# Top-32 attention and a two-layer MLP on one core: weights decoded through a PSUM bank, another cut of the last batch, new priorities

## The chip, the cores and the metric

One Trainium2 chip, one of its cores. The metric is the device time of one execution in microseconds (us), the median of three runs. The core's engines are TensorE (PE), VectorE (DVE), ScalarE (ACT), GpSimd (POOL) and SyncE (SP, which here only issues transfers); each runs its own instructions in their order, and an instruction that must wait holds up all behind it on its engine.

## What is computed

Attention over 4 batches, 8 heads, 576 positions of 64 numbers, in which each query keeps its 32 highest scores; the result, 2304 tokens of 512, goes through two matrices with h * sigmoid(h) between them. All inputs of the attention are fp32; the two weight matrices come as 64-bit floats, for the factor that scales them makes them so.

```python
def _attn_ref(q, k, v):
    scores = scale * np.matmul(q, k.transpose(0, 1, 3, 2))
    kth = np.partition(scores, -top_k, axis=-1)[..., -top_k:-top_k + 1]
    mask = scores >= kth
    scores = np.where(mask, scores, -1000000000.0)
    scores = scores - np.max(scores, axis=-1, keepdims=True)
    attn = np.exp(scores)
    attn = attn / (np.sum(attn, axis=-1, keepdims=True) + 1e-09)
    return np.matmul(attn, v).astype(np.float32)
...
def _moe_ref(x, w_in, w_out):      # x: 2304 x 512, w_in: 512 x 2048, w_out: 2048 x 512
    h = x @ w_in
    g = h * (1.0 / (1.0 + np.exp(-h)))
    return (g @ w_out).astype(np.float32)
```

## The kernel before

**Attention.** Heads go in pairs (four per batch, `pr`). A group is a batch's stretch of query blocks for one pair (`CUTS`: blocks i0 to i1 of 128 queries, and a tail of 64 or not). A tile is 128 queries of one head against 576 keys, 144 tiles in all. For each tile TensorE makes the scores in two halves (L489, or L493 and L494 from batch 1 on), ScalarE copies them to SBUF (L511), VectorE takes the eight highest of each 72 (L577, eight times), thins them to a pivot (L593, L600), ScalarE (L614, L618) and GpSimd (L617) use the pivot to build a row whose eight highest (L619, VectorE) hold the 32nd score. ScalarE makes the exponentials (L534), VectorE masks them and sums them (L540), TensorE transposes them (L644) and, once per chunk of up to 320 queries, multiplies them with the values (L731). VectorE multiplies that with the inverse sums (L739, called the product of a chunk here), ScalarE casts the result to a shortened fp32 (L758) and GpSimd subtracts that from the full one (L270), so that both parts go into the MLP.

**MLP.** The 2304 tokens are nine blocks of 256. A block can start when all four pairs' chunks that cover it have gone through L758 and L270: block 0 needs the first four products L739, block 1 the first eight. For each of the 16 slices of 128 hidden columns TensorE makes three products of 256 columns four times (L798, L799, L800), ScalarE tanh (L804), VectorE the product with h (L807), ScalarE and GpSimd the two parts (L810, L270), and TensorE three products of 512 columns twice (L837 to L839) into two accumulator banks of PSUM (`accs`, banks 6 and 7). Blocks 7 and 8 run together at the end, since batch 3's last group covers both.

**The decode of weights.** Both matrices are 16 tiles each of 128 x 512 64-bit numbers: 32 tiles, loaded by SP (L330). A tile's numbers are pairs of 32-bit words, a low and a high one (`lo_`, `hi_`). The wanted fp32 bits are sign and exponent and 20 bits of mantissa from the high word shifted left by three, and three more bits from the low word. `POOL_SIGN`, a word of 32 bits, picks for each tile one of two ways. For 24 tiles ScalarE turns the low word's upper half into a number near 2 whose last bits are the wanted ones (L348), takes the sign of the high word (L351), GpSimd multiplies the two (L352) and VectorE joins the shifted high word to it by exclusive or (L343). For 8 tiles VectorE shifts and masks (L367) and joins sign and low bits in two further passes (L343 twice). Behind either, ScalarE casts the fp32 tile to its high part (L379) and GpSimd subtracts (L270). Block 0 reads w_in from these tiles; for later blocks each two slices are stored to memory and loaded again by SP.

```python
op("act:dec", 0.565, low, r=[("r", key)], w=[("g", key)], use=[br] + ub)
op("act:sgn", 0.56, ..., r=[("g", key)], w=[("sg", key)], use=[br, bm])
op("pool:sgn", 1.22, ..., r=[("g", key), ("sg", key)], w=[("t1", key)], use=[bm, br])
op("dve:dec+", 0.602, lambda: stt(hi_(), 3, ALU.logical_shift_left, ALU.bitwise_xor), r=[("t1", key)], w=[("t2", key)], use=[bm, br])
```

**What sets the order.** `Schedule` holds all operations with a planned cost, what they read and write, and the buffers they use; `run` plays them through and writes each engine's instructions in the order in which the plan starts them. Where several are ready on an engine at once the one with the lowest priority number goes first: its tile's number plus an entry of `TUNE` for its kind. PSUM banks and SBUF buffers are given out in the plan too: the kinds `sp` (scores), `tp` (transposes), `h` and `pv` share banks 0 to 5 (`ANY`), and `LIMIT` bounds how many buffers of a kind live at once. A kind that ends in `+`, and GpSimd's own kinds, may not overlap in the plan.

A second emission (`general=True`) stands in a branch that is taken only if a check at the end fails; it does not run here. That check reads both matrices again (L907, L911, L915 on VectorE) behind the attention.

## Time and profile before

| | |
|---|---|
| runs, us | 778.66, 778.24, 777.57; median 778.24 |
| the profiled execution, us | 778.45, its span 776.7 |
| busy us of the span | PE 708.6, DVE 670.4, ACT 634.8, POOL 556.7 |
| busy share | PE 91%, DVE 86%, ACT 82%, POOL 72% |
| chain that ended last, by engine | PE 66%, DVE 17%, ACT 8%, issue 3%, POOL 2%, DMA 2% |
[...]

The busy shares are means over stretches that differ: in the first fortieth parts of the span TensorE is busy two to three tenths, from the eleventh on nearly all the time, while VectorE, ScalarE and GpSimd thin out in the last fifth, where the MLP of the last two blocks is left. TensorE's products overlap, so a TensorE that is shown busy is not for that at its peak. [...]

### The profile page before, as it was taken

Reading aid. Unit: us, or ns where it says so; the run is one execution under the profiler, and the core shown is the slowest. Engines: PE = TensorE matmul, PEld = TensorE weight load, DVE = VectorE, ACT = ScalarE, POOL = GpSimd, SP = SyncE. Lnnn points to the kernel's source line nnn. Section 1 sums busy time; section 2 is a strip of 40 time slices with the busy share of each in tenths; the row PEclk is TensorE's granted clock in tenths of the full one; section 3 lists DMA queues with packets and bytes.
Section 4 is the critical chain, followed back from the end, with each engine's and each line's share of the span. In section 5 each row is a group of like instructions: output and inputs, shape, how many; then the busy total and the mean of one; then the engine's idle time right before and its main releaser. Section 6 shows DMA issues by size and latency. Waiting matters only on the chain.

```text
span 776.7 us, 15935 instructions
## 1 busy us (share of the span) xinstructions
PE 708.6 (91%) x4802; PEld 589.8 (76%) x4802; DVE 670.4 (86%) x2931; ACT 634.8 (82%) x1602; POOL 556.7 (72%) x567
## 2 busy tenths in 40 slices
PE   2327789988999999999999999999999999999996
PEld 2214558865888887788978888888888888899995
DVE  4999999987999998999999989799997888769920
ACT  6888998997999989999989999999979898232222
POOL 7999889999998668787866878777776565222221
PEclk8656799999999999999999999999999999999999
DMA  8804342346754335434642454354323343989701
GB/s 316 299 1 133 120 169 67 138 183 253 290 201 159 128 95 195 158 107 162 221 143 89 158 176 151 112 188 170 138 76 122 144 166 135 385 318 343 289 1 60
DMA packets 41600, 131.29 MB, mean 169 GB/s; under 512 B 9504, under 2 KB 15648, under 8 KB 33312
## 3 DMA queue, kind: packets, MB, share of 16 engines
q1 hardware_dynamic: 41504, 130.17, 46.7%
q8 instruction: 40, 0.66, 0.3%
q14 instruction: 56, 0.46, 0.2%
HBM read 117.05 MB, written 13.11 MB: 168 GB/s over the span
## 4 chain that ended last, share of the span: by engine, by line
PE 66%; DVE 17%; ACT 8%; issue 3%; POOL 2%; DMA 2%; SPq 1%; ACTq 0%; POOLq 0%; DVEq 0%
PE bank L731 8%; PE bank L798 7%; PE bank L799 7%; PE bank L800 7%; PE acc L837 7%; PE bank L644 7%; PE acc L839 6%; PE acc L838 6%; DVE cand L577 4%; PE bank L493 3%; PE bank L494 3%; DVE kth L619 3%; DVE p L540 3%; DVE tg L343 2%; PE bank L491 2%
## 5 line engine op out<-in xcount | busy, mean ns | idle before, releaser
L617 POOL TENSOR_TENSOR s<-s,s 128x576 f32<-128x576 f32 x144 | 217.8, 1513 | 48.0 <-ACT s L614 46.9
L577 DVE MAX8 cand<-s 128x8 f32<-128x72 f32 x1152 | 203.3, 218 | 22.1 <-ACT s L511 21.7
L270 POOL TENSOR_TENSOR gg<-tg,gg 128x512 fp32r<-128x512 f32 (+1 forms) x73 | 98.6, 1352 | 102.3 <-ACT gg L810 101.6
L798 PE MATMUL bank<-big,big 128*128 128x256 f32 x576 | 167.2, 290 | 0.0
L800 PE MATMUL bank<-big,big 128*128 128x256 f32 x576 | 162.2, 282 | 0.2 <-POOL big L270 0.2
L799 PE MATMUL bank<-big,big 128*128 128x256 f32 x576 | 162.1, 281 | 0.0
L614 ACT ACTIVATE s<-s,piv 128x576 f32<-128x576 f32 x144 | 113.6, 789 | 10.2 <-DVE piv L593 9.5
L540 DVE SCALAR_TENSOR_TENSOR p<-s,kth,p 128x576 f32<-128x576 f32 x128 | 117.9, 927 | 3.7 <-ACT p L534 3.1
L619 DVE MAX8 kth<-s 128x8 f32<-128x583 f32 x144 | 109.3, 759 | 13.5 <-POOL s L617 12.5
L511 ACT ACTIVATE s<-bank 128x288 f32<-128x288 f32 x288 | 106.7, 426 | 12.9 <-PE bank L489 6.2
L798 PEld LDWEIGHTS bank<-big,big 128*128 128x128 f32 x576 | 109.1, 189 | 8.4 <-issue 4.2
L644 PE MATMUL bank<-ident,p 128*128 128x128 f32 x576 | 81.9, 281 | 33.9 <-DVE p L540 33.6
L799 PEld LDWEIGHTS bank<-big,big 128*128 128x128 f32 x576 | 109.4, 190 | 3.0
L800 PEld LDWEIGHTS bank<-big,big 128*128 128x128 f32 x576 | 109.1, 189 | 0.6 <-POOL big L270 0.6
L837 PE MATMUL acc<-wo,gg 128*128 128x512 f32 x256 | 109.3, 427 | 0.0
L644 PEld LDWEIGHTS bank<-ident,p 128*128 128x128 f32 x576 | 68.0, 144 | 47.4 <-DVE p L540 34.5
L839 PE MATMUL acc<-wo,gg 128*128 128x512 f32 x256 | 101.2, 395 | 1.9 <-POOL gg L270 1.8
L838 PE MATMUL acc<-wo,gg 128*128 128x512 f32 x256 | 100.8, 394 | 0.0
L534 ACT ACTIVATE p<-s,stat 128x576 f32<-128x576 f32 x128 | 98.7, 792 | 1.6 <-POOL stat L544 1.5
L731 PE MATMUL bank<-pt,s 128*64 128x256 f32 (+4 forms) x720 | 93.7, 374 | 0.0
L804 ACT ACTIVATE tg<-bank 128x512 f32<-128x512 f32 (+1 forms) x73 | 43.1, 592 | 58.9 <-PE bank L800 58.5
L656 ACT COPY pt<-bank 128x384 f32<-128x384 f32 x192 | 85.1, 487 | 6.0 <-PE bank L644 5.8
(105 smaller groups left out, 1568.0 us busy)
## 6 DMA issues: line engine op xcount, KB each, us to landing
big<-scr SPq DMA_DIRECT2D x56, 1024.0 KB, 4.9
s<-in_vx_dram SPq DMA_DIRECT2D x36, 288.0 KB, 4.6
big<-in_w_in_dram SPq DMA_DIRECT2D x16, 512.0 KB, 4.4
big<-in_w_out_dram SPq DMA_DIRECT2D x16, 512.0 KB, 6.6
scr<-big SPq DMA_DIRECT2D x8, 1024.0 KB, 4.1
p<-in_w_in_dram SPq DMA_DIRECT2D x16, 512.0 KB, 6.4
p<-in_w_out_dram SPq DMA_DIRECT2D x16, 512.0 KB, 7.0
out_dram<-tg SPq DMA_DIRECT2D x18, 256.0 KB, 2.6
```

Of the source, the lines that this page charges most:

```text
L540: nc.vector.scalar_tensor_tensor(out=x["p"], in0=x["s"], scalar=thr[e], in1=x["p"], op0=ALU.is_ge, op1=ALU.mult, accum_out=den[:, e:e + 1])
L577: nc.vector.max(out=d["cand"][:, 8 * c:8 * c + 8], in_=d["s"][:, 72 * c:72 * c + 72])
L617: op("pool:f", 1.36, lambda: nc.gpsimd.tensor_tensor(out=d["f"][:, 0:S], in0=d["f"][:, 0:S], in1=d["s"], op=ALU.mult), r=both, w=[("f", t) ...
L619: op("dve:mx8", 0.675, lambda: nc.vector.max(out=kth[:, 143 - t:151 - t], in_=d["f"][:, 0:S + 7]), r=[("f", t), ("pad", t)], w=[("thr", t) ...
L644: nc.tensor.transpose(d["tp", r][0:w, o0:o0 + 128], st[key][:, c0:c0 + w], ident)
L731: nc.tensor.matmul(ck.pv[64 * h:64 * h + 64, 0:n], v, ck.pt[:, 4 if j == 4 else 5 * h + j, 0:n], start=(j == 0), stop=(j == 4), skip_group ...
L798: nc.tensor.matmul(h, wh, x[:, 0, kk, :], start=(kk == 0), stop=False)
L799: nc.tensor.matmul(h, wh, x[:, 1, kk, :], start=False, stop=False)
L800: nc.tensor.matmul(h, wl, x[:, 0, kk, :], start=False, stop=(kk == 3))
L837: nc.tensor.matmul(a, d["gg"][:, 0, ts], wo[:, m, 0, :], start=(m == 0), stop=False)
L838: nc.tensor.matmul(a, d["gg"][:, 0, ts], wo[:, m, 1, :], start=False, stop=False)
L839: nc.tensor.matmul(a, d["gg"][:, 1, ts], wo[:, m, 0, :], start=False, stop=(m == NM - 1))
```

## The change

All 32 tiles are now decoded in one way. ScalarE writes the low word's number into a PSUM bank (kind `dec`, which may take the two accumulator banks while they are free, or any of the six shared ones), VectorE joins the shifted high word to it in the bank, and a second VectorE pass joins the sign and writes the fp32 tile to SBUF. The sign pass of ScalarE, the product of GpSimd, the shift of VectorE and `POOL_SIGN` are gone. Batch 3's queries are cut as those of batches 1 and 2, (0, 2) and (2, 4) with the tail, in place of (0, 3) and (3, 4) with the tail: a chunk of 256 and one of 320 queries per pair, where there were 256, 128 and 192. The priorities `TUNE`, the limits of buffers and three constants of the plan (`SLOP`, `DMA_SLOP`, and the general branch's `big.ro`) have other values, so the order on all engines is another throughout.

```diff
-TUNE = {"cand": 76.5, "cert": -38.5, "dec": 0.5, ... "whi": 42, "wi": 22, "wlo": 21, "wload": -20.5, "xhi": -14, "xlo": -8.5}
+TUNE = {"cand": 26.5, "cert": -30, "dec": 3.5, ... "whi": -31, "wi": -8, "wlo": 16.5, "wload": 64.5, "xhi": -36, "xlo": -2.5}
...
-CUTS = [...] + [((0, 2, False), (2, 4, True))] * (NB - 2) + [((0, 3, False), (3, 4, True))]
+CUTS = [...] + [((0, 2, False), (2, 4, True))] * (NB - 1)
...
-LIMIT = {"big.ri": 1, "big.ro": 18, "big.w": 6, "p.c": 16, "p.k": 4, "p.p": 16, "r.n": 19, "r.s": 37, "r.x": 20, "s": 6, "s.e": 40, "s.f": 4, "s.k": 1, "s.v": 1}
+LIMIT = {"big.ri": 1, "big.ro": 2, "big.w": 5, "p.c": 33, "p.k": 4, "p.p": 24, "r.n": 25, "r.s": 27, "r.x": 10, "s": 6, "s.e": 44, "s.f": 9, "s.k": 1, "s.v": 1}
...
-POOL_SIGN = 0xeff5a7ee
 ANY = [b(i) for i in range(6)]
-PSUM = dict(sp=ANY, tp=ANY, h=ANY, pv=ANY, acc0=[b(6)], acc1=[b(7)], acc2=ANY, acc3=ANY)
+PSUM = dict(dec=[b(6), b(7)] + ANY, sp=ANY, tp=ANY, h=ANY, pv=ANY, acc0=[b(6)], acc1=[b(7)], acc2=ANY, acc3=ANY)
...
-            if not general and POOL_SIGN >> 2 * m + "io".index(kind) & 1:
+            if not general:
+                bd = buf("dec", key, "dec" + kind)
+
                 def low():
                     tiles_()
-                    nc.scalar.activation(out=lo_().bitcast(F32), in_=d["r"].bitcast(U16)[:, :, 1], func=AF.Copy, scale=7.49 / 65535 * 2.0 ** -22, bias=2.0)
-
-                op("act:dec", 0.565, low, r=[("r", key)], w=[("g", key)], use=[br] + ub)
-                op("act:sgn", 0.56, lambda: nc.scalar.activation(out=d["top"], in_=hi_().bitcast(F32), func=AF.Sign), r=[("g", key)], w=[("sg", key)], use=[br, bm])
-                op("pool:sgn", 1.22, lambda: nc.gpsimd.tensor_tensor(out=d["top"], in0=d["top"], in1=lo_().bitcast(F32), op=ALU.mult), r=[("g", key), ("sg", key)], w=[("t1", key)], use=[bm, br])
-                op("dve:dec+", 0.602, lambda: stt(hi_(), 3, ALU.logical_shift_left, ALU.bitwise_xor), r=[("t1", key)], w=[("t2", key)], use=[bm, br])
+                    d["low"] = bank("dec", key)[:, 0:CW]
+                    nc.scalar.activation(out=d["low"], in_=d["r"].bitcast(U16)[:, :, 1], func=AF.Copy, scale=7.49 / 65535 * 2.0 ** -22, bias=2.0)
+
+                def join(out, scalar, op0):
+                    nc.vector.scalar_tensor_tensor(out=out.bitcast(I32), in0=hi_(), scalar=scalar, in1=d["low"].bitcast(I32), op0=op0, op1=ALU.bitwise_xor)
+
+                op("act:dec", 0.565, low, r=[("r", key)], w=[("g", key)], use=[br, bd] + ub)
+                op("dve:dec", 0.602, lambda: join(d["low"], 3, ALU.logical_shift_left), r=[("g", key)], w=[("t1", key)], use=[br, bd])
+                op("dve:dec", 0.602, lambda: join(d["top"], -0x80000000, ALU.bitwise_and), r=[("t1", key)], w=[("t2", key)], use=[bm, br, bd])
```

Lines from 400 on have a number higher by one in the kernel after (L739 is L740, L798 is L799); the decode's pass of ScalarE is L350 there, the join L353, ScalarE's cast L380, GpSimd's subtraction L269.

On VectorE, near the start of the program, the first join of before stands among the rows of the second and third tile (`cand`, `m`, `piv` and `c` are the pivot search, `kth` the 32nd score, `gg` an SBUF tile, `big` raw weights):

```order
L577 MAX cand_199<-s_169 128x8 x2
L343 SCALAR_TENSOR_TENSOR gg_160<-big_111,gg_160 128x512
L619 MAX kth<-s_185 128x8
L577 MAX cand_199<-s_169 128x8 x3
L577 MAX cand_226<-s_193 128x8
```

In the kernel after, the same place (`acc` and `bank` are PSUM banks, `p` the masked exponentials):

```order
L541 SCALAR_TENSOR_TENSOR p_206,stat<-s_125,kth,p_206 128x576
L594 MAX m_212<-c_0_217 128x8
L353 SCALAR_TENSOR_TENSOR acc_81<-big_135,acc_81 128x512
L601 MATCH_REPLACE c_0_217<-m_212,c_0_217 128x64
L353 SCALAR_TENSOR_TENSOR gg_220<-big_135,acc_81 128x512
L594 MAX piv_172<-c_0_217 128x8
L620 MAX kth<-s_215 128x8
L353 SCALAR_TENSOR_TENSOR acc_82<-big_143,acc_82 128x512
L353 SCALAR_TENSOR_TENSOR bank_78<-big_135,bank_78 128x512
L353 SCALAR_TENSOR_TENSOR gg_226<-big_143,acc_82 128x512
```

A tile's two joins stand as a pair, in and out of one bank, the first of them later than before, behind a first mask; then joins follow each other.

On VectorE, at the end of the decode before, the eighth product of a chunk (L739, `r_2156`) stands between the last joins:

```order
L343 SCALAR_TENSOR_TENSOR tg_2109<-big_2030,tg_2109 128x512
L807 SCALAR_TENSOR_TENSOR tg_2066<-tg_2066,bank_79 128x512
L600 MATCH_REPLACE c_0_2129<-m_2123,c_0_2129 128x64
L739 TENSOR_TENSOR r_2156<-bank_78,r_2028 128x256
L593 MAX piv_2161<-c_0_2129 128x8
L343 SCALAR_TENSOR_TENSOR tg_2109<-big_2030,tg_2109 128x512
L343 SCALAR_TENSOR_TENSOR gg_2121<-big_2030,gg_2121 128x512
```

After, the last joins there are these, and the eighth product (L740) stands 55 rows further down:

```order
L353 SCALAR_TENSOR_TENSOR bank_80<-big_1840,bank_80 128x512
L578 MAX cand_1912<-s_1752 128x8
L353 SCALAR_TENSOR_TENSOR tg_1928<-big_1840,bank_80 128x512
L620 MAX kth<-s_1910 128x8
L353 SCALAR_TENSOR_TENSOR bank_76<-big_1840,bank_76 128x512
L578 MAX cand_1912<-s_1752 128x8
L353 SCALAR_TENSOR_TENSOR gg_1962<-big_1840,bank_76 128x512
```

The last of the weights are joined ahead of the eighth product, no longer behind it.

Ahead of that eighth product VectorE's rows are, by line, 38 L343, 8 L367, 33 L540, 280 L577, 104 L593, 70 L600, 34 L619, 9 L697, 7 L739, 7 L807 before; after they are 64 joins, 34 masks, 293 L577, 108 L593, 72 L600, 34 L619, 9 L697, 7 L739, 8 L807 (by the numbers of before).

## Rows read from the trace of the kernel before

**Rows 1.** Busy time of each engine by stretches (start:end and length in us, then per engine busy us and number of instructions; PEclk is the granted clock as a share of full speed, here 2.4 GHz).

```profile
0.00:20.00 20.00, 5.75 (x16) 4.04 (x16) 10.21 (x57) 13.23 (x29) 14.81 (x30) 0.86 0.88 315
20.00:140.00 120.00, 79.94 (x423) 58.58 (x423) 117.79 (x473) 105.24 (x246) 113.18 (x92) 0.80 0.37 128
140.00:188.60 48.60, 43.93 (x285) 33.59 (x284) 41.40 (x168) 43.42 (x102) 46.55 (x43) 0.96 0.50 184
0.00:188.60 188.60, 129.62 (x721) 96.21 (x722) 169.40 (x696) 161.90 (x375) 174.54 (x163) 0.85 0.46 162
...
200.00:650.00 450.00, 448.63 (x3229) 378.79 (x3229) 412.45 (x2002) 423.75 (x1114) 337.70 (x366) 1.00 0.44 154
```

**Rows 2.** The chain that ended last, in order of time: start us, us, engine, what it writes, line, and how many instructions the piece holds.

```profile
29.48 0.69 DVE cand L577 x5
...
45.83 3.47 DVE tg L343 x2
...
56.37 1.76 DVE p L540 x2
...
150.56 2.58 POOL big L270 x2
```

**Rows 3.** Instructions in order of time, around the turn to token block 1 and (last two rows) two products of 512 columns late in the span: start us, us, engine, line, operation, out<-in, shapes.

```profile
188.15 0.41 DVE L739 TENSOR_TENSOR r<-bank,r 128x256 f32<-128x256 f32 x1
...
188.62 0.68 DVE L343 SCALAR_TENSOR_TENSOR tg<-big,tg 128x512 int32<-128x512 int32 x1
...
189.32 1.17 POOL L270 TENSOR_TENSOR big<-r,big 128x256 fp32r<-128x256 f32 x1 [0.57 <-ACT big L758]
...
200.06 0.28 PE L798 MATMUL bank<-big,big 128*128 128x256 f32 x1
...
758.25 0.39 PE L837 MATMUL acc<-wo,gg 128*128 128x512 f32 x1
758.47 0.39 PE L838 MATMUL acc<-wo,gg 128*128 128x512 f32 x1
```

**Rows 4.** Busy time from 0 to 200 us of the instructions of one line each, in this order: L348 and L351 (ScalarE), L352 (GpSimd), L343 and L367 (VectorE). All instances of these lines lie in the stretch.

```profile
0.00:200.00 200.00, 15.70 (x24) 0.85 0.47 167
0.00:200.00 200.00, 15.72 (x24) 0.85 0.47 167
0.00:200.00 200.00, 37.59 (x24) 0.85 0.47 167
0.00:200.00 200.00, 38.01 (x40) 0.85 0.47 167
0.00:200.00 200.00, 5.00 (x8) 0.85 0.47 167
```

**Rows 5.** Single lines (durations in ns as least/median/most), the group of L804 (busy us, mean ns), and two rows in order of time in which a join and a GpSimd subtraction run beside each other.

```profile
L807 DVE SCALAR_TENSOR_TENSOR tg<-tg,bank x73: 421/681/690, 119.5 to 765.9; 128x512 f32<-128x512 f32 x71, 128x256 f32<-128x256 f32 x2
...
L343 DVE SCALAR_TENSOR_TENSOR tg<-big,tg x22: 673/750/1892, 22.7 to 188.6; 128x512 int32<-128x512 int32 x22
...
L804 ACT ACTIVATE tg<-bank 128x512 f32<-128x512 f32 x71 | 42.4, 598 | 54.7 <-PE bank L800 54.3
...
45.83 3.46 DVE L343 SCALAR_TENSOR_TENSOR tg<-big,tg 128x512 int32<-128x512 int32 x2
...
47.02 1.72 POOL L270 TENSOR_TENSOR wo<-tg,wo 128x512 fp32r<-128x512 f32 x1
```

**Rows 6.** VectorE's groups by line from 0 to 200 us: busy us, mean ns of one | idle us before them.

```profile
L540 DVE SCALAR_TENSOR_TENSOR p<-s,kth,p 128x576 f32<-128x576 f32 x32 | 30.7, 959 | 0.4 <-ACT p L534 0.3
...
L593 DVE MAX8 m<-cand 128x8 f32<-128x64 f32 x37 | 8.0, 216 | 0.5
```

**Rows 7.** VectorE's waits, from 140 to 188.6 us and (last row) in the first 20 us: what waited, for what, total us, times, longest.

```profile
DVE tg L343 <- POOL tg L352: 1.7, 2, 1.2
DVE kth L619 <- POOL s L617: 1.6, 2, 1.2
DVE tg L807 <- ACT tg L804: 1.2, 1, 1.2
DVE cand L577 <- ACT s L511: 0.9, 1, 0.9
DVE rd L697 <- POOL rd L694: 0.6, 1, 0.6
...
DVE cand L577 <- ACT s L511: 8.9, 4, 5.0
```

**Rows 8.** The chain in order of time again: nine transposes (L644), and sets of twenty rows of L731, the weighted values of a chunk of 320, 256, 128 and 192 queries.

```profile
241.43 0.98 PE bank L644 x9
...
321.31 2.84 PE bank L731 x20
...
606.15 2.31 PE bank L731 x20
...
621.33 1.24 PE bank L731 x20
...
634.73 1.78 PE bank L731 x20
```

**Rows 9.** Instructions in order of time in the first 10 us: issues of transfers on the queue of SP, and ScalarE's first decode pass with what it waited for.

```profile
1.18 1.19 SPq L404 DMA_DIRECT2D p<-in_kx_dram  x2
...
9.00 0.67 ACT L348 ACTIVATE big<-big 128x512 f32<-128x512 uint16 x1 [1.22 <-DMA big<-in_w_out_dram]
```

More of the change, by code (lines that the diff above doesn't have):

```diff
@@ L31 @@
 W_MAX = float(np.uint32(0x47EFFFFF).view(np.float32))
-CUTS = [((0, 2, False), (2, 4, False), (4, 4, True))] + [((0, 2, False), (2, 4, True))] * (NB - 2) + [((0, 3, False), (3, 4, True))]
+CUTS = [((0, 2, False), (2, 4, False), (4, 4, True))] + [((0, 2, False), (2, 4, True))] * (NB - 1)
 SEGS = [(b, *cut) for b in range(NB) for cut in CUTS[b]]
@@ L57 @@
 PORT_DVE, PORT_POOL = 0.12, 0.05
-DMA_GO, DMA_END, FREE, SLOP, START, ALPHA = 0.65, 0.8, 0.2, 0, 1.5, 0
+DMA_GO, DMA_END, FREE, SLOP, START, ALPHA = 0.65, 0.8, 0.2, 0.05, 1.5, 0
 WINDOW = 4096 / 1.2e3
-DMA_SLOP = 3
+DMA_SLOP = 2
 GAP = {
@@ L300, in emit @@
     def emit(general):
-        own = {"s": SBUF["s"] - 5, "s.f": 1, "s.e": 1, "s.k": 1, "s.v": 2, "p.k": 4, "p.p": 2, "r.x": 1, "r.s": 1, "r.n": 1, "big.ri": 1, "big.ro": 1, "big.w": 2}
+        own = {"s": SBUF["s"] - 5, "s.f": 1, "s.e": 1, "s.k": 1, "s.v": 2, "p.k": 4, "p.p": 2, "r.x": 1, "r.s": 1, "r.n": 1, "big.ri": 1, "big.ro": 2, "big.w": 2}
         S_ = turn[0] = Schedule(own if general else LIMIT)
@@ L309, in bank @@
             i = S_.at[kind, key][0][1]
-            return banks[i]
+            return (banks + accs)[i]
         dw, wi, raws = {}, {}, {}
@@ new lines, in split_w, with mag @@
+                op("dve:dec", 0.602, lambda: join(d["low"], 3, ALU.logical_shift_left), r=[("g", key)], w=[("t1", key)], use=[br, bd])
+                op("dve:dec", 0.602, lambda: join(d["top"], -0x80000000, ALU.bitwise_and), r=[("t1", key)], w=[("t2", key)], use=[bm, br, bd])
+            else:
+                def mag():
+                    tiles_()
+                    nc.scalar.activation(out=d["top"], in_=hi_().bitcast(F32), func=AF.Abs)
+                op("act:dec", 0.48, mag, r=[("r", key)], w=[("g", key)], use=[br] + ub)
+                op("dve:dec+", 0.335, lambda: nc.vector.tensor_scalar(out=d["top"], in0=d["top"], scalar1=W_MIN, scalar2=W_MAX, op0=ALU.max, op1=ALU.min), r=[("g", key)], w=[("g1", key)], use=[bm])
@@ L363, in shl @@
                 def shl():
-                    if not general:
-                        tiles_()
                     top = d["top"].bitcast(I32)
-                    nc.vector.tensor_scalar(out=top, in0=top if general else hi_(), scalar1=3, scalar2=0x3FFFFFF8 if general else -0x40000001, op0=ALU.logical_shift_left, op1=ALU.bitwise_and)
+                    nc.vector.tensor_scalar(out=top, in0=top, scalar1=3, scalar2=0x3FFFFFF8, op0=ALU.logical_shift_left, op1=ALU.bitwise_and)
                 op("dve:dec+", 0.335, shl, r=[("g1", key), ("r", key)], w=[("t1", key)], use=[br] + ub)
-                op("dve:dec+", 0.602, lambda: stt(hi_(), -0x40000000 if general else -0x80000000, ALU.bitwise_and, ALU.bitwise_xor), r=[("t1", key)], w=[("t2", key)], use=[bm, br])
+                op("dve:dec+", 0.602, lambda: stt(hi_(), -0x40000000, ALU.bitwise_and, ALU.bitwise_xor), r=[("t1", key)], w=[("t2", key)], use=[bm, br])
```

10 lines of the change are left out of this document (2 added, 8 removed).

## The prediction

> **What bounds the kernel now.** I read the busy time by stretches first, then the chain that ended last, then the waits of single engines. The stretches [rows 1] part the span in two. From 200 to 650 us TensorE is busy 448.6 of 450 us; from there on TensorE's own work sets the pace. Up to 188.6 us it is busy 129.6 us only, while VectorE is busy 169.4, GpSimd 174.5 and ScalarE 161.9 us; from 20 to 140 us VectorE is busy 117.8 of 120. So ahead of 200 us three engines are full at once, VectorE most of all, and TensorE waits for them. The chain in order of time [rows 2] says the same: up to 60 us its long pieces are VectorE's, joins of the decode (L343) and masks (L540); from 150 us it goes over to GpSimd and ScalarE. What is gained ahead of 200 us is kept, if TensorE behind it does the same work at the same pace; what is gained later on another engine than TensorE is worth little.
>
> The point that I use as a clock is where TensorE turns to token block 1 (of 256 tokens, nine in all): its first product starts at 200.06 us [rows 3], and 576.6 us of the span of 776.7 follow. It needs the eighth product of attention and softmax sums (L739, at 188.15 us, seen by the stretch that I end at 188.6), whose cast (ScalarE) and subtraction (GpSimd) end at 190.5 (189.32 + 1.17). In the kernel before TensorE came only at 200.06 because block 0 was not done: the last join of weights but one starts at 188.62 us [rows 3], behind the eighth product, and ScalarE and GpSimd still have to split what it gives.
>
> **The change, the decode.** Before, 24 of the 32 tiles take two ScalarE passes (L348, L351), a GpSimd product (L352) and one VectorE join (L343); 8 take a shift (L367) and two joins. By their busy sums [rows 4] that is 15.7 + 15.7 = 31.4 us on ScalarE (0.65 each), 37.6 on GpSimd, 38.0 + 5.0 = 43.0 on VectorE. After, all 32 take one ScalarE pass into a PSUM bank and two VectorE joins out of it.
> - GpSimd loses 24 products: -37.6 us.
> - ScalarE: 32 passes. None of before writes PSUM; nearest are the same pass into SBUF (0.65) and L804, which reads a bank (0.598, [rows 5]). 32 x 0.65 = 20.8, so -10.6 us (-12.3 at 0.598).
> - VectorE: 64 joins. Their price decides. The 40 of before take 0.95 us each on the mean (38.0 / 40), though the faster ones take 0.67; they rise to 1.89 while GpSimd works beside them: at 45.83 us two take 3.46 us, with a GpSimd row of 1.72 us beside the second [rows 5]. The nearest row for a join with an operand in a bank is L807, 128x512 as well: 0.681 median, 0.690 at most in 73, though GpSimd is busy through most of the kernel; L807 is never slowed. I take 0.68: 64 x 0.68 = 43.5 us, +0.5 against 43.0. Lower end 0.673, the fastest join of that group of before: 43.1, nothing. Upper end 0.95, were the new joins slowed as the old ones: 60.8, +17.8. Of the ends 0.68 is the row with the nearest operands; no row writes a bank from VectorE, so the first join of each pair is the less certain.
>
> [...]
>
> **Where the time goes to.** What VectorE must do ahead of the eighth product is counted from the order: 64 joins in place of 38 joins and 8 shifts, and, moved ahead of it, 13 L577, 4 L593, 2 L600, one mask L540 and one L807. The decode is 64 x 0.68 = 43.5 against 38 x 0.95 + 5.0 = 41.1, so +2.4; the moved work is 13 x 0.14 (the piece of five in 0.69 of [rows 2]), 6 x 0.22 and 0.96 [rows 6] and 0.68, together 4.8. VectorE's work is then 169.4 + 7.2 = 176.6 us. Upon it come idle times: before, 19.2 us (188.6 - 169.4). 9.8 of these fall in the first 20 us, 2.2 up to 140, and 7.2 between 140 and 188.6 [rows 1]. Of these last, 3.9 us are waits for GpSimd (L352 itself 1.7) and 2.1 for ScalarE [rows 7], the two engines that lose 37.6 and 10.6 us of work. If they all go, 13.2 us stay; if none, 19.2. I take the middle, 16.2: part of these waits will have other causes then. The eighth product starts at 176.6 + 16.2 = 192.8; its cast and its subtraction end 2.3 us behind its start (190.49 - 188.15), so block 1 can start at 195.1 us, not 200.06: **5.0 us** earlier (8.0 to 2.0 for the ends). The last join now stands 55 rows ahead of that product on VectorE (before, behind it), so block 0 no longer sets the point. It costs nothing on the path that ScalarE and GpSimd still cast and subtract 32 tiles: both have room now.
>
> TensorE has also done more by then. The order sets 12 more 128x512 products ahead of block 1's first (0.22 to 0.23 us from start to start, 2.7 us), less 5 transposes (nine in 0.98, so 0.5), 2 score products (288 columns, 0.13 each by those of 512) and one set of weighted values for 64 queries (a quarter of 2.31, 0.6) [rows 3, 8]: +1.3 us. Together **6.3 us** ahead.
>
> **The last batch.** Its queries were cut 256 + 128 and 192, now 256 and 320. By the chain's pieces of twenty L731 [rows 8], 2.31 + 1.24 + 1.78 = 5.33 us per head pair become 2.31 + 2.84 = 5.15: 0.18 x 4 = **0.7 us** less on TensorE, which is the bound there. Four chunks less also spare small work on ScalarE and VectorE off the path. The wait behind the last chunk is covered: before, TensorE has block 6's last products to do between the last L731 and block 7, and by the order it has a little more of them now.
>
> **Loads.** The first weight is now behind 14 transfers on SP, not 3; at 0.4 to 0.6 us an issue [rows 9] that is about 6 us later, so it lands near 15 us: before, ScalarE starts on it at 9.00 us. VectorE's own rows ahead of its first join are now 25 L577, 8 L593, 5 L600, an L619 and a mask, at the durations above (L619 not over a mask's 0.96) some 8 us, and they can't start before the first scores, which are no earlier than before: 14 us at least. That hides all but about 1 us, which lies within the idle time above. With that cover gone it would cost up to 6 us.
>
> **Priorities.** All the order behind block 1 is anew. Priced at nothing, for TensorE does the same products there; both ends open: VectorE idles 37.6 us and ScalarE 26.3 us between 200 and 650 [rows 1], and TensorE's waits there can shrink or grow by some us.
>
> **The sum.** 6.3 + 0.7 = 7.0 us. The profiled execution took 778.45 us for a span of 776.7; the median of the runs is 778.24, 0.2 below it. So the profiled execution would come to 771.45, and the median to 778.24 - 7.0 = **771.2 us**; with the ends of the idle time 768 to 774.
>
> **Rivals.**
> 1. *VectorE takes the place of the others, no gain.* It is as full as before (+7.2 us ahead of the eighth product). With all 19.2 us of idle time, and 2 us more as late weights or held banks stop it (six shared banks also serve scores, transposes and block 0 once the two accumulator banks are taken), block 1 starts at 176.6 + 21.2 + 2.3 = 200.1 us, and only the 2.0 us of TensorE's own are left at most: 776.7 to 779. For it: 117.8 of 120 us busy. Against: its waits past 140 us name the relieved engines. 0.13.
> 2. *The joins are slowed still: slower.* Place: VectorE up to the eighth product, which bounds there. The gain of 7.0 us is used up at 64 x 0.11, so from 0.79 us a join on; slower by over 0.2% (1.6 us) from 0.81. At 0.95, the mean of before, it is 64 x 0.27 = 17.3 us, less 7.0: 788; with the first of each pair alone at 1.0 or more, 781 and up. For it: no row in which VectorE writes a bank, and GpSimd works on beside the joins with 32 subtractions of weights. Against: L807 under GpSimd load. 0.12.
> 3. *The new order loses where TensorE is the bound*, say 10 to 15 us of TensorE waits more between 200 and 680 us: 781 to 786. For it: VectorE is busy 412.5 and ScalarE 423.8 of the 450 us from 200 on, so a wait has little slack to hide in. Against: that stretch has no part of the decode. 0.08.
> 4. *More is gained*: idle time at 13.2 us or less, and TensorE's waits behind 200 us shrink by some us too: 757 to 766. For it: of the 9.8 us in the first 20 us VectorE waits 8.9 for ScalarE's copies of scores [rows 7], and the first decode passes stand behind them now. 0.09.
>
> The forecast, 766 to 776, keeps 0.58. Faster by over 0.2% (what a measurement of this kernel can tell from no change): 0.58 + 0.09 = 0.67; within it 0.13; slower 0.12 + 0.08 = 0.20. For 8 in 10 the range takes in rival 1, the lighter half of rival 2 and the nearer half of rival 4: 762 to 782.
>
> **What would show it.** Right: no L352; new joins at 0.66 to 0.70 us, also beside GpSimd; block 1's first product (L799) at 191 to 198 us; GpSimd's busy sum near 515 us (37.6 less, and some small work of four chunks), ScalarE's near 621, VectorE's within 8 us of 670.4; the time from block 1's start to the end near 575 us. Wrong: joins at 0.8 or more, block 1 at 200 or later, or a longer stretch from there to the end.

## The result, and the profile after

| | before | after |
|---|---|---|
| median of four runs, us | 778.45 (777.57 to 779.8) | 761.66 (760.98 to 762.16) |
| profiled execution, span, us | 778.45, 776.7 | 761.32, 759.5 |
| block 1's first product (L799), us | 200.06 | 181.12 |
| from there to the end of the span, us | 576.6 | 578.4 |
| busy us: PE, DVE, ACT, POOL | 708.6, 670.4, 634.8, 556.7 | 710.0, 664.3, 623.4, 499.5 |

The ratio is 0.9782 [0.9765, 0.9799]: faster, by 16.8 us where 7.0 were forecast. The forecast of 771.2 us is 9.5 us off, and the time lies 0.3 us below its range. In the profiled execution all that is gained shows ahead of block 1: 18.9 us there, and 1.8 us of it are given back behind it.

The stretches of the kernel after answer to [rows 1]; the eighth product starts at 178.5 us in place of 188.15. Columns: start:end and length, then busy us (instructions) of PE, PEld, DVE, ACT and POOL, the granted clock, DMA share, GB/s.

```profile
0.00:20.00 20.00, 6.88 (x19) 4.67 (x19) 12.71 (x58) 12.37 (x27) 10.74 (x27) 0.89 0.84 285
20.00:140.00 120.00, 94.40 (x497) 68.88 (x499) 119.49 (x510) 109.22 (x261) 82.83 (x84) 0.86 0.44 160
140.00:178.50 38.50, 37.64 (x260) 28.50 (x256) 37.59 (x171) 37.13 (x87) 34.76 (x36) 1.00 0.74 266
0.00:178.50 178.50, 138.92 (x773) 102.05 (x774) 169.80 (x737) 158.72 (x374) 128.34 (x146) 0.89 0.55 197
...
260.00:272.00 12.00, 8.74 (x53) 6.91 (x52) 11.26 (x64) 11.83 (x32) 9.13 (x12) 0.84 0.29 98
272.00:650.00 378.00, 377.65 (x2636) 314.46 (x2636) 343.37 (x1647) 351.96 (x920) 274.52 (x286) 1.00 0.43 151
```

The fourth row is the result. VectorE's work ahead of the eighth product is 169.80 us, nearly what it was: 169.40 up to 188.6 us [rows 1], and 168.95 without the product itself, up to its start at 188.15. Its idle time there is 178.5 - 169.8 = 8.7 us, where it was 19.2. By the first three rows the idle time is 7.3, 0.5 and 0.9 us; before, 9.8, 2.2 and 7.2. GpSimd has fallen from 174.5 to 128.3 us. What VectorE still waits for there (engine, line, waited for: total us, times, longest), the first two rows all in the first 20 us; they answer to [rows 7]:

```profile
DVE cand L578 <- ACT s L512: 5.4, 2, 5.1
DVE acc L353 <- ACT acc L350: 1.0, 1, 1.0
...
DVE r L740 <- PE bank L732: 0.7, 1, 0.7
DVE p L541 <- ACT p L535: 0.4, 1, 0.4
```

No wait for GpSimd is left, and the last thing the eighth product (L740) waits for is now TensorE. The turn to block 1 (answers to [rows 3]), rows of single engines in order of time:

```profile
178.49 0.42 DVE L740 TENSOR_TENSOR r<-bank,r 128x256 f32<-128x256 f32 x1 [0.72 <-PE bank L732]
...
178.94 0.41 ACT L759 CAST big<-r 128x256 fp32r<-128x256 f32 x1 [0.89 <-DVE r L740]
...
180.28 0.74 POOL L269 TENSOR_TENSOR big<-r,big 128x256 fp32r<-128x256 f32 x1
...
181.12 0.28 PE L799 MATMUL bank<-big,big 128*128 128x256 f32 x1
```

The new decode, by line (ns least/median/most), answers to [rows 4, 5]:

```profile
L350 ACT ACTIVATE bank<-big x21: 602/629/670, 16.8 to 160.3; 128x512 f32<-128x512 uint16 x21
...
L353 DVE SCALAR_TENSOR_TENSOR bank<-big,bank x21: 672/687/701, 17.5 to 161.0; 128x512 int32<-128x512 int32 x21
L353 DVE SCALAR_TENSOR_TENSOR tg<-big,bank x17: 661/673/682, 21.5 to 159.8; 128x512 int32<-128x512 int32 x17
```

Joins that write the bank and joins that only read it cost nearly the same, and none goes over 0.701 us; those of before went up to 1.89. Instructions in order of time, VectorE and then GpSimd, show it, and something else:

```profile
37.90 0.80 DVE L541 SCALAR_TENSOR_TENSOR p<-s,kth,p 128x576 f32<-128x576 f32 x1
...
38.62 0.69 DVE L353 SCALAR_TENSOR_TENSOR bank<-big,bank 128x512 int32<-128x512 int32 x1
39.22 0.22 DVE L578 MAX8 cand<-s 128x8 f32<-128x72 f32 x1
39.37 0.66 DVE L353 SCALAR_TENSOR_TENSOR tg<-big,bank 128x512 int32<-128x512 int32 x1
...
43.26 0.67 DVE L353 SCALAR_TENSOR_TENSOR tg<-big,acc 128x512 int32<-128x512 int32 x1
43.84 0.69 DVE L353 SCALAR_TENSOR_TENSOR acc<-big,acc 128x512 int32<-128x512 int32 x1
44.44 0.23 DVE L578 MAX8 cand<-s 128x8 f32<-128x72 f32 x1
...
37.91 2.05 POOL L618 TENSOR_TENSOR s<-s,s 128x576 f32<-128x576 f32 x1
```

The two joins at 38.62 and 39.37 lie beside GpSimd's row of 37.91 to 39.96 (the second but for its last 0.07 us) and are not slowed. That row is long, 2.05 us against 1.49 on the mean of its group, but it began beside a mask (37.90, two operands in SBUF), and the joins are not what made it so: the eight rows of its group that lie beside joins and beside no mask take 1.42 us on the mean. And a join's row is longer than the place it takes: the join of 38.62 ends at 39.31, but the next row starts at 39.22; from 43.26 to 43.84 and 44.44 the starts are 0.58 and 0.60 us apart. Behind all 64 joins the next row starts a median of 0.08 us before the join's end. So a sum of durations counts more than the time that the rows cover.

Behind block 1, TensorE runs out of work once, as block 2 is not ready (row 260 to 272 above: 8.74 of 12 us, while ScalarE is busy 11.83 and VectorE 11.26). Then its granted clock falls: it is 0.50 of full speed from 268.2 to 274.8 us, and 1.00 again from 275. (The profile gives the clock as this share only; no run shows the 2.4 GHz of [rows 1].) Two stretches of 5 us there, and TensorE's waits from 260 to 272 us:

```profile
265.00:270.00 5.00, 2.75 (x14) 2.10 (x14) 4.86 (x20) 5.00 (x15) 4.64 (x7) 0.81 0.03 7
270.00:275.00 5.00, 4.86 (x23) 4.86 (x24) 5.00 (x23) 4.70 (x11) 4.64 (x5) 0.51 0.19 52
```

```profile
PE bank L495 <- POOL q L269: 1.6, 1, 1.6
PE bank L709 <- ACT r L702: 0.9, 1, 0.9
PE bank L645 <- DVE p L541: 0.8, 1, 0.8
```

### The profile page after: what moved, and what is told of

Read it like the earlier page. It is cut to its first block, busy times and chain, and to the rows that moved or that the text cites. A ratio compares the mean times of both kernels' runs of the same rounds, so it can differ in the third digit from the quotient of the medians.

```text
span 759.5 us, 15736 instructions
## 1 busy us (share of the span) xinstructions
PE 710.0 (93%) x4722; PEld 585.3 (77%) x4722; DVE 664.3 (87%) x2939; ACT 623.4 (82%) x1574; POOL 499.5 (66%) x531
## 4 chain that ended last, share of the span: by engine, by line
PE 76%; DVE 15%; ACT 3%; DMA 2%; issue 2%; SPq 1%; DVEq 0%; ACTq 0%
PE bank L732 9%; PE bank L799 8%; PE acc L838 8%; PE bank L800 8%; PE bank L801 8%; PE bank L645 8%; PE acc L840 7%; PE acc L839 7%; DVE cand L578 3%; PE bank L494 3%; DVE p L541 3%; PE bank L495 3%; DMA big<-in_w_in_dram 2%; PE bank L492 2%; DVE kth L620 2%
## 5 line engine op out<-in xcount | busy, mean ns | idle before, releaser
L618 POOL TENSOR_TENSOR s<-s,s 128x576 f32<-128x576 f32 x144 | 214.2, 1489 | 83.6 <-ACT s L615 71.8
L578 DVE MAX8 cand<-s 128x8 f32<-128x72 f32 x1152 | 208.3, 219 | 16.2 <-ACT s L512 15.4
L799 PE MATMUL bank<-big,big 128*128 128x256 f32 x576 | 168.9, 293 | 0.0
L269 POOL TENSOR_TENSOR gg<-tg,gg 128x512 fp32r<-128x512 f32 (+1 forms) x73 | 99.7, 1367 | 93.7 <-ACT gg L811 93.1
L541 DVE SCALAR_TENSOR_TENSOR p<-s,kth,p 128x576 f32<-128x576 f32 x128 | 121.7, 953 | 0.7 <-ACT p L535 0.4
L799 PEld LDWEIGHTS bank<-big,big 128*128 128x128 f32 x576 | 109.3, 190 | 8.5 <-issue 3.7
L645 PE MATMUL bank<-ident,p 128*128 128x128 f32 x576 | 84.8, 284 | 26.0 <-DVE p L541 21.3
L732 PE MATMUL bank<-pt,s 128*64 128x256 f32 (+2 forms) x648 | 89.5, 388 | 0.0
```

The source lines that it names most:

```text
L541: nc.vector.scalar_tensor_tensor(out=x["p"], in0=x["s"], scalar=thr[e], in1=x["p"], op0=ALU.is_ge, op1=ALU.mult, accum_out=den[:, e:e + 1])
L578: nc.vector.max(out=d["cand"][:, 8 * c:8 * c + 8], in_=d["s"][:, 72 * c:72 * c + 72])
L618: op("pool:f", 1.36, lambda: nc.gpsimd.tensor_tensor(out=d["f"][:, 0:S], in0=d["f"][:, 0:S], in1=d["s"], op=ALU.mult), r=both, w=[("f", t) ...
L645: nc.tensor.transpose(d["tp", r][0:w, o0:o0 + 128], st[key][:, c0:c0 + w], ident)
L732: nc.tensor.matmul(ck.pv[64 * h:64 * h + 64, 0:n], v, ck.pt[:, 4 if j == 4 else 5 * h + j, 0:n], start=(j == 0), stop=(j == 4), skip_group ...
L799: nc.tensor.matmul(h, wh, x[:, 0, kk, :], start=(kk == 0), stop=False)
```

## The experiments

The theory was that the time ahead of block 1 comes from the work taken off GpSimd and ScalarE (A); the rivals, that it is the new order (B), or the end of the slowing of joins (C). Ratios are against the kernel before on the same chip, whose medians were 781.54, 779.82 and 779.86 us in the three groups of runs. "Work" and "idle" are VectorE's ahead of the eighth product; block 1 is the start of its first product; "rest" is from there to the end of the span. The last three columns are from one profiled execution of each kernel.

| kernel | us | ratio, interval | block 1 | work, idle | rest |
|---|---|---|---|---|---|
| before | 778.45 | 1 | 200.1 | 169.0, 19.2 | 576.6 |
| after | 761.66 | 0.9782 [0.9765, 0.9799] | 181.1 | 169.8, 8.7 | 578.4 |
| e1 new decode alone | 775.62 | 0.9934 [0.9915, 0.9953] | 186.3 | 170.7, 13.2 | 587.3 |
| e7 new decode and cut | 769.33 | 0.9868 [0.9837, 0.9898] | 186.1 | 171.5, 12.3 | 580.8 |
| e2 after, old decode | 798.92 | 1.0235 [1.0206, 1.0264] | 213.7 | 188.2, 22.9 | 585.0 |
| e3 after, old cut | 769.75 | 0.9879 [0.9842, 0.9917] | 183.9 | 170.6, 10.7 | 583.7 |
| e12 after, three groups | 761.69 | 0.9762 [0.9736, 0.9787] | 183.6 | 170.7, 10.3 | 576.8 |
| e4 after, joins in SBUF | 789.46 | 1.012 [1.0091, 1.0148] | 209.2 | 198.8, 7.8 | 576.9 |
| e5 GpSimd work back | 775.51 | 0.9918 [0.9888, 0.9947] | 196.2 | 172.4, 21.1 | 577.7 |
| e6 ScalarE work back | 768.09 | 0.9848 [0.9815, 0.988] | 189.5 | 170.1, 16.9 | 577.6 |
| e8 VectorE work added | 787.74 | 1.0096 [1.0064, 1.0128] | 195.9 | 181.2, 12.0 | 590.3 |
| e9 the same, order kept | 773.75 | 0.9918 [0.989, 0.9945] | 195.1 | 183.5, 9.0 | 576.1 |
| e10 priorities off by 0.5 | 774.0 | 0.9922 [0.9897, 0.9947] | 181.7 | 167.6, 11.6 | 590.4 |
| e11 priorities off by 1 | 763.26 | 0.9787 [0.9764, 0.9811] | 186.0 | 170.6, 11.3 | 574.9 |

**e1: the new decode alone.** The kernel before with the new decode; priorities, cut and limits of before (the constants `SLOP` and `DMA_SLOP` are those of after).

```diff
-TUNE = {"cand": 26.5, "cert": -30, "dec": 3.5, ...}
+TUNE = {"cand": 76.5, "cert": -38.5, "dec": 0.5, ...}
-CUTS = [...] + [((0, 2, False), (2, 4, True))] * (NB - 1)
+CUTS = [...] + [((0, 2, False), (2, 4, True))] * (NB - 2) + [((0, 3, False), (3, 4, True))]
-LIMIT = {..., "big.ro": 2, "big.w": 5, "p.c": 33, ...}
+LIMIT = {..., "big.ro": 18, "big.w": 6, "p.c": 16, ...}
```

> The new decode in the kernel before, with the priorities, cuts and buffer limits of before (the plan's two slack constants are those of the kernel after; with those of before no plan is found). Theory A, relief: VectorE's idle time ahead of the eighth product comes from GpSimd and ScalarE, whose work the decode cuts, so most of the 16.8 us comes from the decode alone: idle time under 12 us (19 before), block 1 at 182 to 188 us, 762 to 767 us. Rival B, the new order: the priorities bring most; the decode alone gives the 5 to 7 us of the forecast or less: block 1 at 193 us or later, 770 us or more. Joins at 0.68 us by both.

Block 1 came 13.8 us earlier with the order's numbers as before, most of the 18.9 us. So the lead is the decode's, with the two constants, which are not told apart from it. But the rest grew by 10.7 us, and the time fell by 0.66% only. Theory A had block 1 right and missed the idle time (13.2 us, not under 12) and the time (775.62, not 762 to 767).

**e2: the old decode with the rest new.** The block of the decode in the kernel after is that of before; its priorities, cut and limits are kept.

```diff
-                op("act:dec", 0.565, low, r=[("r", key)], w=[("g", key)], use=[br, bd] + ub)
...
+                op("pool:sgn", 1.22, ..., r=[("g", key), ("sg", key)], w=[("t1", key)], use=[bm, br])
+                op("dve:dec+", 0.602, ..., r=[("t1", key)], w=[("t2", key)], use=[bm, br])
```

> The kernel after with the decode of before (two ScalarE passes, GpSimd product and join for 24 tiles), priorities, cuts and limits of after (the plan's slack constants are those of before; with those of after no plan is found). Theory A: nearly all of the gain is gone, 774 to 785 us, VectorE idle 15 us or more ahead of the eighth product. Rival B: most of the gain stays, 764 to 770 us.

Slower than before by 2.35%, past what A expected, with VectorE's work 19.2 us up and its idle time 3.7: the new priorities and cut are no gain by themselves; with the old decode the same numbers are worse than the old ones. B as a cause of its own falls. An order fitted to the old decode with the new cut was not tried. The work is no matter of waits. The 40 old joins are 1.07 us each there, not 0.96, and all 40, not 38, stand ahead of the product: they cover 5.8 us more. The masks, which also have two operands in SBUF, are 1.11 us each, not 0.96, and 35 in place of 33: they cover 6.7 more. The rest is other rows moved ahead of the product.

**e4: the joins in SBUF.** ScalarE's pass and the joins use the low words of the raw tile; the bank is held as before, but nothing is in it. The plan is the same.

```diff
-                    d["low"] = bank("dec", key)[:, 0:CW]
+                    bank("dec", key)
+                    d["low"] = lo_().bitcast(F32)
```

> The kernel after with the same plan, but ScalarE's pass writes back into the raw tile in SBUF and both joins work there; the bank is held in the plan and not used. Tells what PSUM itself is worth: GpSimd's work is as small as in the kernel after, but the joins have two SBUF operands. If joins are slowed by GpSimd's instructions (rival C: the gain is the end of that slowing), their mean is 0.85 to 0.95 us, VectorE has 10 to 17 us more ahead of the eighth product, and the time is 772 to 779 us. By theory A alone (less GpSimd work, so little to collide with) the mean join stays under 0.75 us and the time is 762 to 766 us.

The joins take 1.12 us on the mean and the time is 789.46 us, both past what C expected. By line, and in order of time on VectorE and GpSimd:

```profile
L354 DVE SCALAR_TENSOR_TENSOR tg<-big x23: 668/680/1909, 25.9 to 185.9; 128x512 int32<-128x512 int32 x23
L354 DVE SCALAR_TENSOR_TENSOR gg<-big x9: 680/1607/1886, 15.6 to 189.0; 128x512 int32<-128x512 int32 x9
```

```profile
47.31 1.88 DVE L354 SCALAR_TENSOR_TENSOR tg<-big 128x512 int32<-128x512 int32 x1
...
46.72 1.92 POOL L619 TENSOR_TENSOR s<-s,s 128x576 f32<-128x576 f32 x1
```

The whole loss is VectorE's work, 198.8 against 169.8 us, with the idle time no larger: 64 x (1.124 - 0.680) = 28.4 us of the 29.0. A join of two SBUF operands beside GpSimd's row of 1.92 us takes 1.88; the joins with an operand in a bank took 0.701 at most in the kernel after. This is C, and it is larger than the 0.95 us a join of before that the prediction took as its upper end.

**e5, e6: the work back on one engine.** The kernel after with 24 products on GpSimd (e5), or 24 sign passes on ScalarE (e6), that nobody reads, planned at no cost. All other instructions stand in the same order.

```diff
+                if 0xeff5a7ee >> 2 * m + "io".index(kind) & 1:
+                    op("pool:sgn-", 0.0, lambda: nc.gpsimd.tensor_tensor(out=lo_().bitcast(F32), in0=hi_().bitcast(F32), in1=hi_().bitcast(F32), op=ALU.mult), r=[("g", key)], use=[br])
```

```diff
+                if 0xeff5a7ee >> 2 * m + "io".index(kind) & 1:
+                    op("act:sgn", 0.0, lambda: nc.scalar.activation(out=lo_().bitcast(F32), in_=hi_().bitcast(F32), func=AF.Sign), r=[("g", key)], use=[br])
```

> The kernel after with 24 GpSimd products of 128x512 more, one beside each of the 24 tiles that had one, whose results nobody reads; planned at no cost so that the order stays nearly as it is. Theory A: VectorE waits again for GpSimd and its masks are slowed: block 1 8 to 15 us later, 768 to 776 us. Rival B (order) and rival C (joins): within 3 us of the kernel after, since the joins in a bank are not slowed and the order is the same.

> The kernel after with 24 ScalarE sign passes of 128x512 put back that nobody reads, planned at no cost; nothing else is changed. They are 24 x 0.65 = 15.6 us of ScalarE. If the relief of ScalarE is a part of the gain as that of GpSimd was, VectorE's idle time ahead of the eighth product rises from 8.7 to 12 us or more, block 1 starts at 185 us or later and the time is 765 to 772 us. Rival, only the relief of GpSimd counts: block 1 stays within 2 us of 181.1 and the time within 2 us of 761.7.

Block 1 is 15.1 us later with GpSimd's work back and 8.4 with ScalarE's; the idle time rises by 12.4 and 8.2, the work by 2.6 and 0.3. The 2.6 are mostly masks slowed beside GpSimd, 1.07 us each in place of 1.01. As the same order reaches block 1 up to 2.8 us later in other runs (e3 and e12 below), some 12 to 15 us of the first and 6 to 8 us of the second are sure. Both reliefs count. VectorE's longest waits ahead of the eighth product, e5 and then e6:

```profile
DVE cand L580 <- ACT s L514: 5.5, 2, 5.2
DVE acc L353 <- ACT acc L350: 4.9, 2, 4.1
DVE rd L700 <- POOL rd L697: 4.5, 2, 3.3
DVE kth L622 <- POOL s L620: 2.1, 3, 0.9
```

```profile
DVE bank L353 <- ACT bank L350: 5.6, 10, 1.0
...
DVE acc L353 <- ACT acc L350: 2.9, 3, 2.1
```

With GpSimd loaded, waits for GpSimd's rows are back; with ScalarE loaded, it is the first pass of the decode itself (L350) that comes late, ten times.

**e8, e9: work added on VectorE.** 24 joins more that nobody reads; in e8 as operations of their own, in e9 issued by the second join's operation, so that all other instructions keep their order.

```diff
+                def second():
+                    join(d["top"], -0x80000000, ALU.bitwise_and)
+                    if 0xeff5a7ee >> 2 * m + "io".index(kind) & 1:
+                        join(d["low"], -0x80000000, ALU.bitwise_and)
```

> The kernel after with 24 more VectorE joins in a bank that nobody reads, planned at no cost. Two joins that stand behind each other start 0.60 us apart, though each row is 0.68 long: 24 x 0.60 = 14.4 us of VectorE. If VectorE alone sets when block 1 starts, it starts at 181.1 + 14.4 = 195.5 us and the time is 774 to 778 us. Rival, the idle time that is left (8.7 us) and the engines beside it take part of it up: block 1 at 190 us or earlier and 770 us or less. By the rows' full length it would be 16.3 us and 778 us.

> The kernel after with the same 24 more VectorE joins that nobody reads, now issued right behind the second join of their tile and without a place of their own in the plan, so that every other instruction keeps its place on its engine. If VectorE sets when block 1 starts, it starts at 181.1 + 24 x 0.60 = 195.5 us, from there to the end it is 578 us as in the kernel after, and the time is 774 to 778 us. Rival, the 12 us that the earlier run of these joins lost behind block 1 came from the joins and not from its other order: 785 us or more.

The 24 rows of e9 have a mean of 0.683 us, 16.4 together. VectorE's busy time ahead of the eighth product, 192.4 us here, rose by 183.44 - 169.80 = 13.6 us, 0.57 each, and block 1 by 14.0:

```profile
0.00:192.40 192.40, 140.14 (x773) 101.19 (x774) 183.44 (x760) 161.57 (x374) 127.94 (x146) 0.88 0.52 183
```

VectorE's work ahead of block 1 goes into its start one for one, at the spacing of the rows. The span grew by 11.7 us; the time, 773.75, is 0.25 us below the 774 to 778 expected. In e8 block 1 came as late, but 12 us more were lost behind it (rest 590.3), and the time, 787.74, missed both that were expected. e9 has the same joins and a rest of 576.1, so it is e8's other order that lost them, and the rival falls.

**e3, e7, e12: the cut of the last batch.** e3 is the kernel after with the old cut, e7 is e1 with the new one, and e12 has three groups in the kernel after.

```diff
-CUTS = [...] + [((0, 2, False), (2, 4, True))] * (NB - 1)
+CUTS = [...] + [((0, 2, False), (2, 4, True))] * (NB - 2) + [((0, 2, False), (2, 3, False), (3, 4, True))]
```

> The kernel after with the query blocks of the last batch cut as before (256 + 128 and 192 in place of 256 and 320). If the cut is worth what TensorE's work says (0.18 us for each of four head pairs), the time is 761.7 + 0.7 = 762.4 us, within 1.5 us of it, and the whole of the difference lies behind 580 us: block 1 starts within 1 us of 181.1. Rival, the new priorities fit only the new cut: TensorE then waits more behind block 5 and the time is 766 us or more.

> The kernel before with the new decode and the new cut, but the old priorities and buffer limits. The new decode alone gave 775.6 us with block 1 at 186.3. If the cut is worth 0.7 us this gives 774.9 us, within 2 us, and the other 13 us down to 761.7 are the priorities and limits. Rival, the new cut is what an order behind block 1 lacked: 768 us or less, and from block 1 to the end 580 us or less in place of 587.3.

> The kernel after with the last batch cut in three, (0, 2), (2, 3) and (3, 4) with the tail: chunks of 256, 128 and 192 queries, as many chunks as in the old cut, but the first group ends at query 256 as in the new one. If the new cut gains because block 6 of the MLP needs only 256 queries of each pair of the last batch where it needed 384, so that TensorE has that block's products early, block 6 starts within 4 us of 585.8 us, TensorE waits less than 1.5 us between 550 and 650 us, and the time is 761.7 + 0.7 = 762.4 us, up to 764.5. Rival, the gain is the smaller number of chunks: 768 us or more, as with the old cut.

The cut is worth far more than 0.7 us: 0.97% (7.6 us) between e3 and the kernel after, 0.66% (5.1 us) between e1 and e7. Both times lie near or in what the rivals said, and block 1 of e3 came 2.8 us later where 1 was allowed. Block 1 is at the same place in e1 and e7, so that gain lies behind it. e12 says why. It has the old number of chunks and costs nothing. Stretches 550 to 600 and 600 to 650 us of e3, what TensorE waited for there, and the same stretches of e12:

```profile
550.00:600.00 50.00, 47.42 (x339) 38.93 (x336) 43.70 (x228) 43.69 (x118) 34.95 (x44) 1.00 0.25 84
600.00:650.00 50.00, 48.74 (x380) 42.14 (x380) 44.14 (x192) 43.41 (x121) 32.50 (x40) 1.00 0.40 138
```

```profile
PE bank L732 <- ACT pt L657: 1.4, 2, 0.7
PE bank L709 <- ACT r L702: 1.1, 1, 1.1
PE bank L494 <- ACT pt L657: 1.1, 1, 1.1
```

```profile
550.00:600.00 50.00, 50.00 (x352) 42.91 (x352) 41.49 (x204) 40.54 (x107) 34.12 (x43) 1.00 0.47 165
600.00:650.00 50.00, 50.00 (x399) 42.97 (x399) 37.92 (x182) 42.13 (x122) 29.76 (x40) 1.00 0.36 127
```

Block 6's first products in e3 and in e12 (585.78 us in the kernel after):

```profile
604.87 0.37 PE L799 MATMUL bank<-big,big 128*128 128x256 f32 x1
```

```profile
585.89 0.28 PE L799 MATMUL bank<-big,big 128*128 128x256 f32 x1
```

Block 6 needs the first group of the last batch from all four pairs, 256 queries each in the new cut and 384 in the old. With the old cut it comes 19 us later, and meanwhile TensorE has only attention to do and waits 3.8 us in these two stretches, 3.6 of them for ScalarE. Of the 5.3 us by which e3's rest is longer than that of after, 4.6 are TensorE's idle time (14.5 against 9.9) and 0.7 its rows. That this is the 0.7 of the prediction is chance, for the rows of after hold the fall of the clock at 268 us, which e3 has not (1.00 from 200 to 300 us): against e12, which has as many chunks and no such fall (a clock of 0.89 up to the eighth product as after, but 0.973 over the span against 0.969), e3's rest is 6.8 us longer, 4.6 idle time and 2.2 rows. Between e1 and e7 TensorE's idle time is the same (10.8 and 11.1 us), though block 6 starts 17.6 us earlier in e7 (591.6 against 609.2), and the gain is in its rows: 3.2 of 6.7 us are those of L732 (73.2 and 70.0 us). What makes the others shorter there stays open, beyond that e1's clock is 0.98 and e7's 1.00 from 200 to 300 us.

**e10, e11: priorities off a little.** Each number of `TUNE` in the kernel after moved at random by 0.5 (e10) or by 1 (e11), up or down.

```diff
-TUNE = {"cand": 26.5, "cert": -30, "dec": 3.5, "ev": -10.5, ...}
+TUNE = {"cand": 26.0, "cert": -30.5, "dec": 3.0, "ev": -10.0, ...}
```

> The kernel after with each number of its table of priorities moved by 0.5 up or down at random; cut, decode and limits as they are. If the order is fitted closely, so that any other order near it loses several us, the time is 765 us or more, and the losses seen with other re-planned kernels say little of what was changed in them. Rival, orders near it are as good: 760 to 763.5 us.

> The same with each number moved by 1 up or down, other signs. If the order is fitted closely: 765 us or more. Rival, orders near it are as good: 760 to 763.5 us.

They split: e10 loses 1.4% (10.9 us), e11 is 0.05% from the kernel after, within either's interval, though block 1 is 5 us later in it. So an order near this one may cost nothing or 11 us, and a difference of that size between two re-planned kernels is not by itself an effect of what was changed. In e10 the loss is behind block 1. From 340 to 370 us:

```profile
340.00:370.00 30.00, 25.50 (x143) 19.55 (x142) 29.62 (x150) 29.03 (x79) 23.05 (x25) 0.83 0.36 128
```

TensorE has used up a block and the next is not there, while VectorE and ScalarE are full, and its clock falls (0.83 on the mean of the stretch, between its levels of 1.00 and 0.50): the same picture as at 260 us in the kernel after. e10 has it once before, from 258 to 275 us, where TensorE is idle 5.1 us and its clock stays at 1.00. Of the 12.0 us by which its rest is longer, 7.3 are TensorE's idle time (17.2 against 9.9); the others, in its rows, stay open.

## Why the prediction was wrong

Its sum was 5.0 + 1.3 + 0.7 = 7.0 us. In the trace block 1 starts 14.0 us earlier than forecast (181.1, not 195.1), and 3.8 us of that are lost behind it (578.4, where 576.6 - 1.3 - 0.7 = 574.6 was meant). Of these, 2.2 are waits: TensorE is idle 9.9 us from block 1 to the end, before 7.7, and the three gaps at 261 to 270 us are 3.3. The others go to the fall of the clock from 268 to 275 us. e9 has the same order of TensorE's rows, 10.0 us of idle time and the same three gaps, but its clock stays at 1.00 in and behind them (its mean of 0.968 over 771.2 us is 24.7 us short of full speed; 24.0 of these lie ahead of the eighth product by its means of 0.88, 0.82 and 1.00 from 0 to 20, 20 to 140 and 140 to 192.4 us), and its rows from block 1 to the end take 566.0 us where those of after take 568.5 (567.0 in e12, with 80 rows more). Its waits of TensorE from 200 to 400 us:

```profile
PE bank L500 <- POOL q L269: 1.6, 1, 1.6
PE bank L650 <- DVE p L546: 1.4, 3, 0.9
PE bank L714 <- ACT r L707: 0.9, 1, 0.9
```

The fall cost 2.5 us by this, more than the others come to: without it TensorE's rows are 2.8 us less than before (568.8), where 1.3 + 0.7 = 2.0 were meant. The same waits came with a fall of the clock and without one, so it is not in the order itself.

The measured time is in the range of rival 4 (757 to 766, at a chance of 0.09). Its first half, idle time at 13.2 us or less, came; its second, fewer waits of TensorE behind 200 us, did not. What the sum had wrong, step by step:

- **VectorE's work, +7.2 forecast, +0.8 measured (169.80 against 168.95): wrong.** This is 6.4 of the 14.0 us. The count of rows was right and the join's price, 0.68 us, was right to 0.001 us. But 64 x 0.68 and the moved rows were added as durations to a busy time (169.4) that counts each moment once. By durations VectorE's rows ahead of the eighth product do grow, from 214.0 to 223.1 us; the time they cover grows by 0.8. e9 gives the price that should have been used: 0.57 to 0.60 us a join. With it the decode is 64 x 0.60 = 38.4 us; the old one, its joins 0.97 us and its shifts 0.63 by their rows and each less 0.075 us for its overlap, is 38 x 0.90 + 8 x 0.55 = 38.6. Not +2.4 but -0.2; in the traces the joins and shifts cover 38.6 us before and 38.7 after. That most of the moved rows (4.8 us) vanish too is rows of L594 and L601, which cover 3.3 us less than L593 and L600 did though six more; why is not tested. In the trace of before, too, the row behind a join starts a median of 0.08 us before the join's end.
- **A small double count.** The prediction's 169.4 and 19.2 us reach to 188.6 us, behind the product, and its 2.3 us from the product to block 1 count from the product's start at 188.15: 0.45 us stand in it twice. The 2.3 measured 2.6. With the 6.4 us above and the 7.5 below this makes the 14.0.
- **Idle time, 16.2 forecast (13.2 to 19.2), 8.7 measured: wrong, and below the low end.** This is 7.5 us. The prediction let the 7.2 us past 140 us shrink at most to nothing and held the 12.0 us ahead of 140 fixed. In e1, with the old priorities, idle is 13.2: 7.8, 1.8 and 3.6 us by the three stretches, so the decode alone took 3.6 us past 140, near the 3.0 of the middle value, and 2.4 ahead of it. The new priorities and limits took another 2.5 to 4.5 (the same order has 10.7 and 10.3 us in e3 and e12). That the relief of GpSimd and ScalarE is the cause was right: e5 and e6 put 12.4 and 8.2 us back.
- **The joins are not slowed: right,** and e4 shows that the change rests on it: without it the kernel is slower than before by 1.2%. The slowing of rival 2 is real where both operands are in SBUF: a join takes 1.12 us on the mean there (e4), and 0.68 with one operand in a bank (the kernel after).
- **The last batch, 0.7 forecast, 5 to 8 us measured: wrong.** TensorE's products were counted and nothing else. That block 6 waits for a whole group of every pair was in the kernel's text, and the new cut lets it start 19 us sooner. In the trace of before TensorE hardly waits there (448.6 of 450 us busy, [rows 1]), so the old cut had no price to be read; that it gets one when TensorE is further ahead fits e3 and e12, but not e1 and e7, where no wait went.
- **Priorities at nothing: wrong.** From e7 to the kernel after it is 0.86% (6.7 us); in the profiled executions 5.0 ahead of block 1 (2.2 and 2.5 by the starts of e3 and e12, which have the same order there), 2.4 behind. e2 shows that they are worth this only with the new decode, and e10 that it hangs on the exact order.
- **Gains ahead of block 1 are kept: wrong where the order isn't made for them.** e1 gives back 10.7 of 13.8 us, e11's 5 us later block 1 costs almost nothing. With the order kept, 84% or more of a delay at block 1 stays in the span (e5 14.4 of 15.1 us, e6 7.6 of 8.4, e9 11.7 of 14.0).

By the steps before, e1, e7, after the parts are 5.1, 5.1 and 6.7 us. The decode's own part is near the 6.3 us forecast by luck, because two errors cancel in it: a lead of 13.8 us, and 10.7 of it given back. GpSimd's busy sum came to 499.5 us, not 515: L352's 37.6 went, and its subtractions (8.7 less), its small rows (some 8 less) and those of L617 (3.6 less) shrank too.

## What to carry to other kernels

Price a row on a full engine by the distance between starts of rows that stand back to back, not by its duration (here 0.60 us a join, not 0.68), before it is set against a busy sum. When an edit relieves engines beside the bound, let all idle time that names them go in the low end, early stretches too. Ask of a cut not only what it saves but which later block it lets start, and before reading a difference between two re-planned kernels as an effect, move the order a little without the change and see how far the time goes.
